# Two transformer layers on one core: heads paired in the score units, attention normalized by VectorE transposes, the bias b2 added on GpSimd, and planner latencies taken from a trace

## The chip, the cores and the metric

The kernel runs on one core of one Trainium2 chip. The metric is the device time of one execution in microseconds (us); lower is better. Each kernel was timed several times in rounds shared with the kernel before; quoted times are medians.

TensorE is the matmul engine, VectorE, ScalarE and GpSimd the others. In profile lines they are PE (PEld its weight loads), DVE, ACT and POOL; SP or SPq is the queue that issues DMAs. PSUM (ps in profile lines) is the memory, in banks, that holds what matmuls write. The granted clock is the share of TensorE's full clock that the profile shows as granted.

## The reference, cut to what matters

```python
def _A_ref(x, wqkv, wo):                 # x: 1 x 2048 x 512, 32 heads of 16, window 256
    q, k, v = split(x @ wqkv)
    scores = einsum("bhqd,bhkd->bhqk", q, k) * 16 ** -0.5
    scores = where(0 <= q_index - k_index < 256, scores, -1e9)
    return (softmax(scores) @ v) @ wo
def _B_ref(x, w1, b1, w2, b2):           # 512 -> 1792 -> 512
    return gelu(x @ w1 + b1) @ w2 + b2
x = x + _A_ref(layernorm(x), ...)        # both layers twice, the same weights
x = x + _B_ref(layernorm(x), ...)
```

## The kernel before

The Python program first records some thousand operations with their data dependencies, then a planner (`_Plan.run`) simulates the five engines with assumed durations and latencies. Its greedy list schedule gives the order in which every engine gets its instructions. On the chip the order is fixed; only semaphores decide when the next instruction starts. So a number in the planner changes no operation, but may change the order of all of them.

```python
class _Plan:
    LAT = {"pe": 230.0, "act": 110.0, "dve": 110.0, "pool": 150.0, "sp": 100.0}   # ns to a dependent
    # in run():  pick the ready operation of best priority whose PSUM banks are free
    #            dur += 98.0 at a mode switch of TensorE, += 1283.0 at a table load of ScalarE
    # ... (cut)
```

Scores are computed in units of 320 queries by 128 keys of one head; the two PSUM halves hold two halves of 64 keys. Probabilities times V (PV) then leaves two partial sums, one for each half, in two PSUM banks. Each V carries a 17th column of ones, so its row 16 is the softmax denominator. The normalization follows:

```python
# reduce: adds the two banks, PSUM -> SBUF
add("dve", e.tensor_reduce(out=OD[:, s], in_=ps[:, two banks].rearrange("p b n -> p n b"), op=ALU.add), ...)
dma(Dc[:, rs] <- OD[Dh : P : 32, s])                 # gather the denominators
add("dve", e.reciprocal(Rc[:, rs], Dc[:, rs]), ...)
dma(scr_r[rs] <- Rc[:, rs])                          # to DRAM
dma(Rn[:, rs] <- scr_r[rs] broadcast to 16 rows)     # and back, one row for each of 16
for r in range(4):
    dma(OD[32*r+16 : 32*r+32, s, 0] <- OD[32*r : 32*r+16, s, 1])   # move the odd heads
add("pool" or "dve", e.tensor_tensor(out=OT[:, bs, c], in0=OD[:, s, 0], in1=Rn[:, rs], op=ALU.mult), ...)
# ... OT feeds the out-projection, then residual, layernorm, MLP
```

The bias b2 is one more matmul (a row of ones times b2) in each of the 32 groups of the second MLP product; then VectorE adds X and PSUM. The mask multiply runs on VectorE or GpSimd, as the planner chooses.

The softmax here doesn't subtract the row's maximum and nothing guards it: scores larger than these inputs give would overflow.

## Time and profile before

557.39 us median (557.38 with the execution that was added when the change was timed). Of the profiled execution:

| what | before |
|---|---|
| span of the profiled run | 551.9 us |
| TensorE busy; span less busy | 484.1; 67.8 us |
| ScalarE, VectorE, GpSimd busy | 423.6, 385.9, 271.1 us |
| granted TensorE clock, mean | 0.969 |

The page of the kernel before, from its first part and from the chain of work that ended last (shares of the span):

```profile
span 551.9 us, 20560 instructions
## 1 busy us (share of the span) xinstructions
PE 484.1 (88%) x9040; PEld 247.1 (45%) x9040; DVE 385.9 (70%) x669; ACT 423.6 (77%) x507; POOL 271.1 (49%) x359
...
PE 39%; DMA 18%; DVE 18%; SPq 12%; ACT 9%; issue 3%; POOL 1%; DVEq 0%; POOLq 0%
```

TensorE is the fullest engine, and yet 30% of the chain is DMA and DMA issue. The middle of the kernel before, 60 to 500 us, by windows (busy us of each engine, instruction counts, granted clock, DMA share):

```profile
core 0: us, PE busy (x) PEld busy (x) DVE busy (x) ACT busy (x) POOL busy (x), PEclk, DMA share, GB/s
60.00:500.00 440.00, 394.41 (x7772) 195.90 (x7773) 320.54 (x557) 356.86 (x416) 229.16 (x272) 0.97 0.12 33
```

The groups of instructions of the kernel before that the change touches (busy us, mean ns of one, idle time before them and what ended it):

```profile
L692 POOL TENSOR_TENSOR E<-E,mask 128x512 bf16<-128x512 bf16 x163 | 192.1, 1187 | 147.1 <-ACT E L678 147.1
L737 DVE TENSOR_REDUCE OD<-ps 128x512 f32<-128x1024 f32 x64 | 77.9, 1217 | 14.9 <-PE ps L726 14.4
...
L754 POOL TENSOR_TENSOR OT<-OD,Rn 128x256 bf16<-128x256 f32 x34 | 25.2, 741 | 61.9 <-DMA Rn<-scr_r 56.8 <-DMA OD<-OD 5.1
L744 DVE RECIPROCAL Rc<-Dc 64x32 f32<-64x32 f32 x64 | 21.6, 338 | 28.6 <-DMA Dc<-OD 28.5
...
L757 DVE TENSOR_TENSOR OT<-OD,Rn 128x256 bf16<-128x256 f32 x30 | 16.0, 534 | 26.8 <-DMA Rn<-scr_r 21.3 <-DMA scr_r<-Rc 3.7 <-DMA OD<-OD 1.8
```

The normalization costs VectorE 77.9 + 21.6 + 16.0 = 115.5 us. The waits of the kernel before that end at the normalized tile OT (us in total, times, longest):

```profile
PEld ps L564 <- POOL OT L754: 8.2, 5, 3.3
...
PE ps L564 <- POOL OT L754: 6.9, 5, 3.2
```

The chain of the last attention group of the kernel before, in order of time (start us, us, what), shows the latency itself:

```profile
516.24 1.80 DMA Dc<-OD
...
518.13 1.43 SPq L751
...
522.14 2.71 DMA Rn<-scr_r
...
524.97 0.43 DVE OT L757
```

The reduce of that group starts at 514.8 us, and the out-projection at 525.46. Only part of this is transfer: from 518.13 to 522.1 us the chain consists of five DMA issues that stand one behind the other in SP's queue, about 4 of the 11 us. The Trainium skill, "DMA: Bandwidth & Descriptors" (Anatomy of one DMA), gives a DMA issued by GpSimd a fixed cost of about 2.0 us, most of it waiting for the write to be confirmed; the DMAs here are issued by SP, and the two pieces, 1.80 and 2.71 us, are of that size.

### The profile page before, as it was taken

How to read it: one execution, taken by the hardware profiler on the slowest of the kernel's cores; microseconds unless marked ns; L12 is line 12 of the kernel's file. 1: busy time of each engine (PE TensorE's matmuls, PEld its weight loads, DVE VectorE, ACT ScalarE, POOL GpSimd, SP SyncE). 2: the span in 40 equal slices, each digit the busy share in tenths (PEclk: the TensorE clock that was granted, in tenths of full speed). 3: DMA queues.
4: the chain of work that ended last, by engine and by line, in shares of the span. 5: the costliest groups of instructions: out<-in, count | busy, mean ns of one | idle time of the engine just before them, and what ended most of it. 6: DMA issues, size and time to landing. Idle time of an engine off the chain costs nothing.

```text
span 551.9 us, 20560 instructions
## 1 busy us (share of the span) xinstructions
PE 484.1 (88%) x9040; PEld 247.1 (45%) x9040; DVE 385.9 (70%) x669; ACT 423.6 (77%) x507; POOL 271.1 (49%) x359
## 2 busy tenths in 40 slices
PE   3895788989878997998998999998999998969997
PEld 2553454545433542545444453445434443434653
DVE  5997986868687666856788686786766675863331
ACT  2788798889877894798869987589757996788542
POOL 6575664646584335643566457562553344532010
PEclk9998799999979997998999999999999999979999
DMA  8901111010111011100111101110111102110100
GB/s 275 297 17 41 43 27 40 23 34 20 36 45 33 14 25 38 37 24 11 37 35 33 30 14 42 34 29 15 45 53 43 32 9 61 45 45 25 51 20 30
DMA packets 37131, 24.93 MB, mean 45 GB/s; under 512 B 16305, under 2 KB 36530, under 8 KB 37042
## 3 DMA queue, kind: packets, MB, share of 16 engines
q1 hardware_dynamic: 37042, 23.62, 14.6%
q8 instruction: 71, 1.16, 0.9%
q14 instruction: 18, 0.15, 0.1%
HBM read 16.26 MB, written 2.62 MB: 34 GB/s over the span
## 4 chain that ended last, share of the span: by engine, by line
PE 39%; DMA 18%; DVE 18%; SPq 12%; ACT 9%; issue 3%; POOL 1%; DVEq 0%; POOLq 0%
PE ps L564 30%; SPq L751 9%; DMA Dc<-OD 7%; DMA Rn<-scr_r 6%; ACT E L678 5%; DMA scr_r<-Rc 5%; DVE OD L737 4%; PE ps L665 4%; PE ps L726 3%; DVE KT L608 2%; DVE E L689 2%; DVE X L573 2%; ACT gT L826 1%; SPq L748 1%; PE ps L548 1%
## 5 line engine op out<-in xcount | busy, mean ns | idle before, releaser
L678 ACT ACTIVATE E<-ps 128x1024 bf16<-128x1024 f32 x320 | 303.6, 1039 | 65.4 <-PE ps L665 65.0
L692 POOL TENSOR_TENSOR E<-E,mask 128x512 bf16<-128x512 bf16 x163 | 192.1, 1187 | 147.1 <-ACT E L678 147.1
L564 PE MATMUL ps<-xnTB,W_sb 128*128 128x512 bf16 (+1 forms) x560 | 114.5, 339 | 7.9 <-DVE gT L814 3.9
L564 PE MATMUL ps<-W_sb,gT 128*128 128x512 bf16 x448 | 120.2, 383 | 0.0
L737 DVE TENSOR_REDUCE OD<-ps 128x512 f32<-128x1024 f32 x64 | 77.9, 1217 | 14.9 <-PE ps L726 14.4
L665 PE MATMUL ps<-QT,KT 32*64 32x320 bf16 (+4 forms) x3072 | 69.8, 265 | 15.5 <-ACT E L678 9.4
L564 PE MATMUL ps<-xnTA,Wqkv_sb 128*128 128x256 bf16 x512 | 70.5, 281 | 6.3 <-DVE xnTA L517 1.7
L564 PEld LDWEIGHTS ps<-xnTB,W_sb 128*128 128x128 bf16 x560 | 50.2, 98 | 51.1 <-DVE gT L814 6.8
L573 DVE TENSOR_TENSOR X<-X,ps 128x512 bf16<-128x512 bf16 x64 | 43.2, 676 | 38.7 <-PE ps L564 38.6
L826 ACT ACTIVATE gT<-ps,b1T 128x512 bf16<-128x512 f32 (+1 forms) x92 | 50.4, 584 | 18.6 <-PE ps L564 18.4
L689 DVE TENSOR_TENSOR E<-E,mask 128x512 bf16<-128x512 bf16 x93 | 53.0, 572 | 14.4 <-ACT E L678 13.7
L665 PEld LDWEIGHTS ps<-QT,KT 32*64 32x64 bf16 x3072 | 29.0, 104 | 69.7 <-ACT E L678 36.0
L564 PEld LDWEIGHTS ps<-W_sb,gT 128*128 128x128 bf16 x448 | 37.7, 98 | 45.2 <-issue 14.7
L726 PE MATMUL ps<-E,Va 64*17 64x192 bf16 (+3 forms) x3840 | 52.2, 238 | 6.5 <-DVE E L689 2.7
L564 PEld LDWEIGHTS ps<-xnTA,Wqkv_sb 128*128 128x128 bf16 x512 | 46.3, 100 | 24.0 <-issue 3.3
L726 PEld LDWEIGHTS ps<-E,Va 64*17 64x17 bf16 x3840 | 42.5, 87 | 29.6 <-issue 13.0
L754 POOL TENSOR_TENSOR OT<-OD,Rn 128x256 bf16<-128x256 f32 x34 | 25.2, 741 | 61.9 <-DMA Rn<-scr_r 56.8
L564 PE MATMUL ps<-Wo_sb,OT 128*128 128x512 bf16 x128 | 36.2, 419 | 9.3 <-POOL OT L754 6.9
L608 DVE TENSOR_TENSOR KT<-ps,parmask 128x1024 bf16<-128x1024 f32 x32 | 38.6, 1213 | 6.8 <-PE ps L564 6.6
L530 DVE BATCH_NORM_STATS2 stat<-X 128x6 f32<-128x512 bf16 x64 | 42.8, 679 | 0.5
L744 DVE RECIPROCAL Rc<-Dc 64x32 f32<-64x32 f32 x64 | 21.6, 338 | 28.6 <-DMA Dc<-OD 28.5
L564 PE MATMUL ps<-Wqkv_sb,xnTA 128*128 128x512 bf16 x128 | 35.4, 393 | 5.1 <-DVE KT L608 3.3
(46 smaller groups left out, 360.8 us busy)
## 6 DMA issues: line engine op xcount, KB each, us to landing
Rn<-scr_r SPq DMA_DIRECT2D x64, 128.0 KB
OD<-OD SPq DMA_DIRECT2D x256, 16.0 KB
W_sb<-in_B_w_dram SPq DMA_DIRECT2D x2, 1792.0 KB
out_dram<-X SPq DMA_DIRECT2D x16, 128.0 KB
Wqkv_sb<-in_A_wqkv_dram SPq DMA_DIRECT2D x3, 512.0 KB
X<-in_A_x_dram SPq DMA_DIRECT2D x1, 1024.0 KB
Dc<-OD SPq DMA_DIRECT2D x64, 8.0 KB
scr_r<-Rc SPq DMA_DIRECT2D x64, 8.0 KB
```

Of the source, the lines that this page charges most:

```text
L530: add("dve", lambda e, B: e.bn_stats(stat6[:, k6, :], X[:, t, :]), 680, reads=["X%d" % t], writes=["st%d" % k6], prio=prio)
L564: r = e.matmul(ps[:, B[g][0], cols], lhsT, rhs, start=st, stop=sp)
L573: add("dve", lambda e, B: e.tensor_tensor(out=X[:, t, :], in0=X[:, t, :], in1=ps[:, B[g][0], :], op=ALU.add), d_psum(512), reads=["X%d" % ...
L608: add("dve", lambda e, B, g=g, i=i: e.tensor_tensor(out=KT[:, kb, :, 2 * i : 2 * i + 2, :].rearrange("p a c q -> p a (c q)"), in0=ps[:, B[ ...
L665: x = e.matmul(ps[HK * h : HK * h + HK, bk[r], o : o + n], KT[rows, kb, par, c, j * P + HK * h : j * P + HK * h + HK], QT[rows, c, q + HK ...
L678: a = (add("act", lambda e, B, g_=g_, gi=gi: e.activation(E[:, 2 * gi : 2 * gi + 2, e0 : e0 + 512], ps[:, B[g_][0] : B[g_][0] + 2, :], AF. ...
L689: add("dve", lambda e, B: e.tensor_tensor(out=Ew, in0=Ew, in1=Mw, op=ALU.mult), d_bf2(8 * HK * n), reads=["E%d%s" % (es, x) for es in ess ...
L692: alt=(("pool", lambda e, B: e.tensor_tensor(out=Ew, in0=Ew, in1=Mw, op=ALU.mult), POOL_M * n, POOL_H),))
L726: x = e.matmul(ps[32 * r : 32 * r + VW, B[g][half], par * 256 + q_lo * HK : par * 256 + q_hi * HK], lhsT, rhs, start=(pi == 0), stop=(pi = ...
L737: add("dve", lambda e, B: e.tensor_reduce(out=OD[:, s, :, :].rearrange("p a q -> p (a q)"), in_=ps[:, B[g][0] : B[g][0] + 2, :].rearrange( ...
L751: dma(lambda e, B, r=r: e.dma_start(OD[32 * r + Dh : 32 * r + 2 * Dh, s, 0, :], OD[32 * r : 32 * r + Dh, s, 1, :]), [ods[r]], reads=["Dc%d ...
L826: gelu_last[0] = add("act", lambda e, B, g=g, fc=fc: e.activation(gT[:, fc, 0:M], ps[:, B[g][0], 0:M], AF.Gelu_apprx_tanh, bias=b1T[:, fc ...
```

## The change

The intent is (N) a normalization without DMA, (B) no b2 matmuls on TensorE, and (P) a planner whose latencies come from a trace.

N: a score unit now holds 64 keys of an even head in one PSUM half and of the odd head in the other, so a head's sum over keys stays in one bank and nothing has to be added. V is also stored with its halves swapped (`Vs`, 64 DMA copies), because the odd head's 64 keys may lie in the other 64 rows. The 64 matmuls by zeros with which the old PV opened some of its sums are gone too. PV's output is transposed in 32x32 blocks by VectorE; then a denominator lies beside its 16 values in one partition, is inverted and multiplied there, and the result is transposed back.

```diff
-  e.tensor_reduce(OD, two banks); dma Dc<-OD; e.reciprocal(Rc, Dc); dma scr_r<-Rc; dma Rn<-scr_r; 4 x dma OD<-OD
-  add("pool", OT = OD * Rn, alt "dve")
+  add("dve", e.transpose(OD[:, s, :], ps[:, two banks, 0:256]), 715, ...)
+  sums = OD[:, s, :].rearrange("p (a k n) -> p a k n", a=2, n=32)
+  add("dve", e.reciprocal(Rc[:, s, :], sums[:, :, :, Dh]), 205, ...)
+  add("dve", Nb = sums[:, :, :, 0:Dh] * Rc broadcast, 360, lock=True, alt=(("pool", norm, 741, 0.0, True),))
+  add("dve", e.transpose(OT[:, bs, c, :], Nb[:, s, :]), 420, ...)
... (score and PV loops by head parity, Vs copies: cut)
```

B:

```diff
-  pe_group(g, [(onesb, b2row, ...)] + [(gT, W2_sb, ...) for fc in range(FC)], ...); residual: X = X + ps
+  add("pool", Xb = X + b2all, 1180, ..., lock=True)
+  pe_group(g, [(gT, W2_sb, ...) for fc in range(FC)], ...);  add("dve", X = Xb + ps, 690, ...)
```

P:

```diff
-    LAT = {"pe": 230.0, "act": 110.0, "dve": 110.0, "pool": 150.0, "sp": 100.0}
+    OVER = {"pe": 0.0, "act": 105.0, "dve": 82.0, "pool": 42.0, "sp": 0.0}      # overlap with the next
+    LAT = {"pe": {"pe": 0.0, "act": 204.0, "dve": 204.0, "pool": 230.0, "sp": 230.0},
+           "act": {"pe": 57.0, ...}, "dve": {"pe": 57.0, ...}, "pool": {...}, "sp": {...}}
+    SWITCH = 96.0;  TABLE = 1400.0
+    # lock=True: such operations of VectorE and GpSimd are kept apart in the plan
... (durations of a dozen operations adjusted by up to 110 ns: cut)
```

## The prediction

> **What bounds the kernel now.** TensorE and ScalarE hold each other. The page gives TensorE 484 of 551.9 us busy (88%), ScalarE 424, VectorE 386, GpSimd 271. Cut into windows: from 60 to 500 us TensorE is busy 394 of 440 us and ScalarE 397, both near 90%; from 0 to 60 TensorE only 41.5 (in 30 to 60 VectorE is the full one, 26.8 of 30); from 500 to 552 TensorE works almost alone (48 of 52). So 45 us of TensorE idle in the middle, 18 at the start and 4 at the end can be attacked. The waits view names them: weight loads of the scores waiting for exp 36 us, ScalarE waiting for scores 65 us, TensorE (weight loads and matmuls) waiting for the normalized tile 15 us. The chain of waits puts 18% on DMA and 12% on DMA issue: sums -> reciprocal -> DRAM -> broadcast -> multiply. At 206.6 us the timeline shows TensorE standing 3.2 us for that.
>
> **What changes, costed from the trace.**
> - Normalization: VectorE now spends 64 x 1217 ns (reduce) + 64 x 338 (reciprocal) + 30 x 534 (multiply) = 115 us; GpSimd 25. After: a transpose out of PSUM, estimated at the 677 ns of the 512-column cast, a reciprocal about 0.2, a bf16 transpose about 0.42, a multiply of 0.4 to 0.53, half of them on GpSimd at 741: about 97 us. The Trainium skill, "VectorE: DVE Perf Modes" (Rules for kernel authors), calls tensor_reduce the slowest VectorE op and the 32x32 transpose the fastest within a bank; the trace agrees on the reduce. VectorE gains 15 to 20 us.
> - Latency from PV to out-projection: about 11 us (last block: reduce starts 514.8, out-projection 525.5) becomes 2 to 3. Its 448 DMAs vanish; 64 V-swap copies come, mostly hidden.
> - TensorE: 32 b2 matmuls at about 0.21 us (estimate: spacing of 512-column matmuls in the timeline) and 64 zero matmuls: minus 8 us. Scores and PV keep counts and columns; pairing heads instead of key halves should not change their speed.
> - GpSimd: plus 32 x about 1.18 us (like its 512-element mask multiply, 1187 ns), so about 305 us busy; some masks go to VectorE. A busier GpSimd also delays VectorE's SBUF operations (mask multiply there averages 572 ns).
> - Planner: order from traced latencies, costed only as a share of the 45 us.
>
> **On the critical path.** DMA latency mostly hides behind other blocks' work; only the stalls count: about 10 us in the middle, 2 to 3 at the start, 3 at the end. TensorE work: 7 of 8 counts. Better order: 8 to 10. ScalarE's 424 us stays, so the middle can't fall far below 410. Sum about 31 us: 526.
>
> **Predicted:** 526 us, range 508 to 545. Chances: faster 0.87, same 0.11, slower 0.02.
>
> **What would show it right.** TensorE busy falls to about 474 and its share rises to 90% or more; DMA leaves the chain; VectorE busy 365 to 375, GpSimd about 305; ScalarE within 10 us of 424; middle ScalarE idle below 8%; out-projection waits near zero; transpose near 0.7 us.
>
> **What would make it wrong.** GpSimd's b2 adds and normalizations delay the tiny layernorm operations on it or slow VectorE, so masks and PV slip; V-swap copies arrive late at the first blocks; the new order has more TensorE mode switches or starves ScalarE; the clock (0.969 now) falls as TensorE gets denser. In the other direction: if the old order was the true cause of the gaps, under 510.

## More of the kernel before

One early execution of the kernel before took 1516.97 us; it is in no ratio, and without it the median of the kernel before would be 557.36 instead of 557.38.

The experiments ran in three rounds on different chips, in which the kernel before took 558.05, 555.28 and 555.44 us, so kernels of different rounds are better compared by their ratios than by their medians.

Pairing in the trace the end of each of the 64 reduces with the end of the matching write of OT gives a median of 11.0 us from PSUM eviction to normalized tile.

## The result, and the profile after

The kernel after takes 538.08 us median (533.73 to 539.45) against 557.38: ratio 0.9655, interval [0.9597, 0.9714]. A ratio here is the mean time of one kernel's fast runs over that of the kernel before in the same rounds, so it is not quite the ratio of the medians quoted. The predicted time was 526, so the range holds the result; of the predicted gain of 31 us, 19 came.

The page of the kernel after, the same parts:

```profile
span 535.7 us, 19845 instructions
## 1 busy us (share of the span) xinstructions
PE 472.1 (88%) x8944; PEld 254.8 (48%) x8944; DVE 387.3 (72%) x739; ACT 427.4 (80%) x514; POOL 292.4 (55%) x376
...
PE 60%; DVE 18%; ACT 18%; issue 2%; POOL 2%; POOLq 0%; DVEq 0%
```

DMA has left the chain, and TensorE's busy time fell by 12.0 us. But the span less TensorE's busy time only went from 67.8 to 63.6 us, and VectorE is as busy as before. The groups of the kernel after that answer to those above:

```profile
L747 DVE STREAM_TRANSPOSE OD<-ps 128x512 f32<-128x512 f32 x64 | 45.4, 710 | 17.2 <-PE ps L737 15.7
...
L837 POOL TENSOR_TENSOR Xb<-X,b2all 128x512 f32<-128x512 bf16 x32 | 37.7, 1179 | 44.3 <-DVE X L841 29.8 <-DVE X L594 14.6
...
L760 DVE STREAM_TRANSPOSE OT<-Nb 128x256 bf16<-128x256 bf16 x64 | 27.8, 434 | 2.4 <-POOL Nb L754 2.0
...
L754 POOL TENSOR_TENSOR Nb<-OD,Rc 128x256 bf16<-128x256 f32 x33 | 22.7, 687 | 9.3 <-DVE Rc L750 8.4 <-DVE statmv L553 0.8
...
L754 DVE TENSOR_TENSOR Nb<-OD,Rc 128x256 bf16<-128x256 f32 x31 | 19.5, 628 | 0.5
...
L750 DVE RECIPROCAL Rc<-OD 128x16 f32<-128x16 f32 x64 | 15.4, 240 | 0.2
```

The normalization now costs VectorE 45.4 + 27.8 + 19.5 + 15.4 = 108.1 us, only 7 less than before. The waits of the kernel after that end at OT:

```profile
PEld ps L585 <- DVE OT L760: 0.9, 4, 0.2
PEld ps L691 <- DVE OT L760: 0.4, 1, 0.4
```

No stall at the out-projection is longer than 0.2 us, where it was 3.3. The same pairing in the trace gives a median of 2.9 us from eviction to normalized tile, where it was 11.0. The middle by windows:

```profile
core 0: us, PE busy (x) PEld busy (x) DVE busy (x) ACT busy (x) POOL busy (x), PEclk, DMA share, GB/s
60.00:500.00 440.00, 399.46 (x7972) 210.88 (x7949) 328.41 (x623) 374.11 (x437) 246.03 (x283) 0.96 0.05 13
```

The mean granted clock was 0.958 (0.969 before), and in the timed runs 0.955 to 0.965.

### The profile page after: what moved, and what is told of

It reads as the page before. It is cut to its first block, busy times and chain, and to the rows that moved or that the text cites. A ratio compares the mean times of both kernels' runs of the same rounds, so it can differ in the third digit from the quotient of the medians.

```text
span 535.7 us, 19845 instructions
## 1 busy us (share of the span) xinstructions
PE 472.1 (88%) x8944; PEld 254.8 (48%) x8944; DVE 387.3 (72%) x739; ACT 427.4 (80%) x514; POOL 292.4 (55%) x376
## 4 chain that ended last, share of the span: by engine, by line
PE 60%; DVE 18%; ACT 18%; issue 2%; POOL 2%; POOLq 0%; DVEq 0%
PE ps L585 46%; ACT E L704 12%; PE ps L737 6%; PE ps L691 6%; DVE KT L629 3%; DVE xn L561 2%; DVE stat L551 2%; ACT gT L820 2%; DVE E L715 2%; PE ps L569 2%; DVE OD L747 2%; DVE gT L817 1%; ACT L820 1%; DVE X L841 1%; DVE X L594 1%
## 5 line engine op out<-in xcount | busy, mean ns | idle before, releaser
L718 POOL TENSOR_TENSOR E<-E,mask 128x512 bf16<-128x512 bf16 x151 | 177.3, 1182 | 143.4 <-ACT E L704 143.1
L585 PE MATMUL ps<-W_sb,gT 128*128 128x512 bf16 x448 | 114.9, 380 | 0.3 <-DVE X L841 0.3
L715 DVE TENSOR_TENSOR E<-E,mask 128x512 bf16<-128x512 bf16 x105 | 66.0, 632 | 27.0 <-ACT E L704 26.8
L691 PE MATMUL ps<-QT,KT 32*64 32x320 bf16 (+4 forms) x3072 | 70.2, 267 | 14.8 <-ACT E L704 8.5
L837 POOL TENSOR_TENSOR Xb<-X,b2all 128x512 f32<-128x512 bf16 x32 | 37.7, 1179 | 44.3 <-DVE X L841 29.8
L747 DVE STREAM_TRANSPOSE OD<-ps 128x512 f32<-128x512 f32 x64 | 45.4, 710 | 17.2 <-PE ps L737 15.7
L737 PE MATMUL ps<-E,Va 64*17 64x64 bf16 (+3 forms) x1920 | 51.0, 240 | 5.8 <-ACT E L704 3.0
L737 PE MATMUL ps<-E,Vs 64*17 64x64 bf16 (+3 forms) x1920 | 51.7, 240 | 0.0
L841 DVE TENSOR_TENSOR X<-Xb,ps 128x512 bf16<-128x512 f32 x32 | 21.8, 681 | 34.1 <-PE ps L585 33.9
L569 PE MATMUL ps<-ident,xn 128*128 128x128 bf16 x256 | 25.9, 230 | 20.3 <-DVE xn L561 9.8
L561 DVE TENSOR_SCALAR xn<-X,statmv,rstd 128x512 bf16<-128x512 bf16 x64 | 41.5, 653 | 2.7 <-POOL rstd L558 2.5
## 6 DMA issues: line engine op xcount, KB each, us to landing
W_sb<-in_B_w_dram SPq DMA_DIRECT2D x2, 1792.0 KB, 14.8
```

The source lines that it names most:

```text
L561: add("dve", lambda e, B: e.tensor_scalar(out=xn[:, s, :], in0=X[:, t, :], scalar1=statmv[:, k, 0:1], scalar2=rstd[:, k : k + 1], op0=ALU. ...
L585: r = e.matmul(ps[:, B[g][0], cols], lhsT, rhs, start=st, stop=sp)
L691: x = e.matmul(ps[HK * par : HK * par + HK, bk[r], o : o + n], KT[rows, kb, par, c, m * HK : m * HK + HK], QT[rows, c, q : q + n], start=T ...
L715: add("dve", lambda e, B: e.tensor_tensor(out=Ew, in0=Ew, in1=Mw, op=ALU.mult), 355 * n, reads=["E%d%s" % (es, x) for es in ess for x in " ...
L718: alt=(("pool", lambda e, B: e.tensor_tensor(out=Ew, in0=Ew, in1=Mw, op=ALU.mult), POOL_M * n, POOL_H, True),))
L737: x = e.matmul(ps[32 * r : 32 * r + VW, B[g][par], q_lo * HK : q_hi * HK], V[rows, (2 * b + m // 2) % VR, c * HC + 2 * r + par, :], E[rows ...
```

## The experiments

The three parts can be separated: N, B and P each on or off makes eight kernels, two of which are before and after. Five of the other six were run. Because the order of all instructions follows from the planner's numbers, controls nudge one number, the planner's cost of a TensorE mode switch, by 4 ns. No operation changes, but every engine gets another order (over a thousand lines of difference in VectorE's and TensorE's lists for the kernel after). Idle is the profiled span less TensorE's busy time; a dash stands where the trace lacks about 100 of TensorE's records, so that its busy time is too small to use. One profiled execution stands for each kernel: that of the kernel before (span 551.9 us) was among its fastest, that of norm_only (device time 536.22 us) its slowest, so differences of idle carry an error of some 3 us.

| kernel | N | B | P | median us | ratio to before | TensorE busy | idle | clock |
|---|---|---|---|---|---|---|---|---|
| before | – | – | – | 557.38 | 1 | 484.1 | 67.8 | 0.969 |
| before_jitter | – | – | – | 552.82 | 0.9931 | 483.4 | 70.6 | 0.975 |
| b2_only | – | yes | – | 552.55 | 0.9924 | 474.4 | 77.0 | 0.966 |
| norm_only | yes | – | – | 533.95 | 0.9594 | 481.3 | 53.0 | 0.981 |
| no_planner | yes | yes | – | 528.82 | 0.9496 | 471.7 | 55.4 | 0.971 |
| no_planner_jitter | yes | yes | – | 528.34 | 0.9506 | 470.2 | 56.7 | 0.977 |
| planner_only | – | – | yes | 567.07 | 1.0169 | 490.9 | 75.1 | 0.948 |
| planner_only_jitter | – | – | yes | 564.87 | 1.0167 | – | – | 0.964 |
| b2_back_on_pe | yes | – | yes | 550.15 | 0.9865 | 484.3 | 64.6 | 0.969 |
| after | yes | yes | yes | 538.08 | 0.9655 | 472.1 | 63.6 | 0.958 |
| after_jitter | yes | yes | yes | 526.99 | 0.9471 | 468.3 | 56.3 | 0.971 |
| after_jitter2 | yes | yes | yes | 525.69 | 0.9458 | – | – | 0.964 |
| before_no_dma | wrong result | – | – | 532.44 | 0.9571 | – | – | 0.981 |
| norm_with_hops | yes, slowed | – | – | 545.78 | 0.9813 | – | – | 0.974 |

Half-widths of the 95% intervals are 0.003 to 0.008.

### planner_only: P alone

```diff
  (kernel before)
- old planner class and durations
+ new planner class, its durations, overlaps and locks
```

> The kernel before with the new planner (traced latencies, overlaps, port locks, durations) alone; normalization by DMA and b2 on TensorE stay. Theory of the prediction (three parts that add): 8 to 10 us faster than before, 547 to 550. Rival 1 (the gain is the removed TensorE work, the order is only noise): within 4 us of before, 553 to 561. Rival 2 (the order is the whole gain): 535 to 542.

Measured: 567.07 us, ratio 1.0169 [1.0116, 1.0221]. None of the three theories expected a loss. On the operations of the kernel before, the new planner costs 9 us instead of gaining 8 to 10.

### no_planner: N and B without P

```diff
  (kernel after)
- new planner class and durations
+ old planner class and durations
```

> The kernel after with the old planner and its old durations; paired heads, transposes and b2 on GpSimd stay. Theory of the prediction: gives back 8 to 10 us, 546 to 549. Rival 1 (removed TensorE work is the gain, order is noise): 536 to 542, TensorE busy about 472. Rival 2 (the order is the whole gain): 553 to 560.

Measured: 528.82 us, 0.9496 [0.9444, 0.9549]. All three theories were wrong in time: without the new planner the changed kernel is faster, by about 1.6% in the ratios. N and B together gain 5.0%, some 28 us, nearly the 31 that were predicted for all three.

### b2_back_on_pe: N and P without B

```diff
  (kernel after)
- add("pool", Xb = X + b2all); X = Xb + ps
+ one b2 matmul in each of the 32 groups; X = X + ps
```

> The kernel after with b2 as 32 matmuls again, no GpSimd add. Theory of the prediction: 7 us slower than after, 545, TensorE busy up by 7 to 12 us, GpSimd busy down by 38. Rival 1 (removed TensorE work is the gain): 8 to 12 us slower, 546 to 550. Rival 3 (the GpSimd adds cost about what the matmuls did, by delaying VectorE and the layernorm): within 3 us of after, 535 to 541, VectorE's mean mask multiply back below 600 ns.

Measured: 550.15 us, 0.9865, TensorE busy 484.3: 12.2 more than after, GpSimd's 258.6 us are 33.8 less. B's gain in this pair, 12 us or 2.1%, equals the busy time removed; rival 1 (546 to 550) comes nearest. Rival 3 predicted under 541 and has no support here: the GpSimd adds did not cost what the matmuls did. But these are two single orders, and orders differ by as much (see the controls), so the pair alone decides little. VectorE's mean mask multiply did not return below 600 ns (637). The adds are not what lengthens it: with them alone (b2_only) it is 574 ns, as before (572); with the new normalization alone (norm_only) it is 662.

### b2_only: B alone

```diff
  (kernel before)
- one b2 matmul in each of the 32 groups; X = X + ps
+ add("pool", Xb = X + b2all); X = Xb + ps
```

> The kernel before with b2 on GpSimd alone. Theory of the prediction: 7 us faster, 550. Rival 1: 8 to 12 us faster, 545 to 549. Rival 3 (GpSimd contention eats it): within 3 us of before, 554 to 560.

Measured: 552.55 us, 0.9924 [0.9873, 0.9975]: 0.8%, 4 us, between the bands of the theory and of rival 3, though TensorE's busy time fell by 9.7 us. Idle rose from 67.8 to 77.0: in this pair half of the removed work (by the medians) or nearly all of it (by the profiles) came back as waiting. Between norm_only and no_planner the same part is worth 0.9594 against 0.9496, 1.0% or some 5.5 us; there busy fell by 9.6 and idle rose by only 2.4. Between b2_back_on_pe and after it is worth 2.1%, and idle did not rise at all (64.6 to 63.6). All three pairs have the same sign, but none is clearly larger than what a change of order alone does (before_jitter 0.7%, the orders of the kernel after 2%). So B is worth 4 to 12 us, and these runs don't tell it closer.

### norm_only: N alone

```diff
  (kernel after)
- new planner, b2 on GpSimd
+ old planner, b2 on TensorE
```

> The kernel before with paired heads and DMA-free normalization alone (old planner, b2 on TensorE). The four runs so far read: b2 on GpSimd gains 5.5 to 12, the new planner costs 9, the normalization gains 17 or more. If the parts add: 528.8 + 5.5 to 12 = 534 to 541. Rival (the normalization's gain is an accident of one order): over 547. TensorE busy about 481 to 484; VectorE busy no lower than 380.

Measured: 533.95 us, 0.9594 [0.9526, 0.9662], inside the additive band. Alone it gains 4.1%, 21 to 23 us, at least as much as the whole change (the intervals of the two ratios overlap). With B already there it gains 4.3% (b2_only to no_planner), under the new planner 3.0% (planner_only to b2_back_on_pe). TensorE's busy time fell by only 2.8 us; its idle time fell by 14.8 (67.8 to 53.0). VectorE's busy time is 387.7 us, 1.8 more than before.

### before_jitter, after_jitter, no_planner_jitter, planner_only_jitter, after_jitter2: the controls

```diff
- mode switch 98 (old planner) or 96 (new planner) ns
+ 94 (before_jitter), 102 (no_planner_jitter), 92 (after_jitter, planner_only_jitter), 100 (after_jitter2)
```

> Control: the kernel before with its mode switch 94 instead of 98 ns. If the constants of the kernel before were tuned to one order, every other order is slower: 560 to 570, and then the 9 us of the new planner alone are the loss of that tuning. If the order is not special: 554 to 560.

> Control: the kernel after with one planner constant nudged, TensorE's mode switch 92 instead of 96 ns; same operations and same costs on the chip, but another order on every engine. If the planner's model is what costs 9 us, this stays at 535 to 541. If the spread of orders is as large as the effect, it lands anywhere in 528 to 548, and the 9 us are not the model's.

> Control: the fast run with the old planner, its mode switch 102 instead of 98 ns. If the old model is really better on the changed kernel: 525 to 533. If 528.8 was a lucky order: 534 or more, as the kernel after.

> Control: the kernel before with the new planner, its mode switch 92 instead of 96 ns. If the new model really fits the old operations worse: 562 to 570. If 567 was an unlucky order, as 538 was for the changed kernel: 548 to 560.

> Control: the kernel after with the mode switch at 100 instead of 96 ns. If 538 was an unlucky order and 527 the usual one: 524 to 532. If orders spread evenly: anywhere in 526 to 542.

Measured: 552.82 (0.9931 [0.985, 1.0012]), 526.99 (0.9471), 528.34 (0.9506), 564.87 (1.0167) and 525.69 us (0.9458). (A first try of no_planner_jitter at 94 ns could not be built: the planner ran into a state where no PSUM bank came free.) Three readings follow.

First, 538.08 us is an unlucky order: two other orders of the same operations under the same model take 526 to 527 us, 11 to 12 less (10 to 11 by the ratios), far outside the spread of the executions of either. The kernel before, nudged, is not slower (below both its bands), so it was not tuned to one best order.

Second, on the changed kernel the two models do not differ in what these orders can tell: 528.8 and 528.3 with the old one; 538.1, 527.0 and 525.7 with the new one. The conclusion drawn from no_planner alone, that the new model costs 9 us there, falls.

Third, on the old operations both orders of the new model are 1.7% slower, so there the loss is probably more than luck, though two orders against two do not prove it. With N and b2 on TensorE the new model is slower too (norm_only 0.9594, b2_back_on_pe 0.9865), one order each. Why it is so was not found.

What an unlucky order looks like: the kernel after by windows around a starved stretch.

```profile
core 0: us, PE busy (x) PEld busy (x) DVE busy (x) ACT busy (x) POOL busy (x), PEclk, DMA share, GB/s
180.00:217.60 37.60, 35.44 (x652) 18.18 (x650) 26.11 (x54) 33.06 (x41) 20.01 (x27) 1.00 0.04 10
217.60:231.30 13.70, 9.21 (x302) 5.46 (x295) 8.48 (x16) 12.52 (x14) 6.70 (x8) 0.51 0.01 2
231.30:252.00 20.70, 20.13 (x245) 10.07 (x243) 14.07 (x29) 17.45 (x21) 6.57 (x10) 0.99 0.04 8
```

From 217.6 to 229 us the order gives TensorE nothing but scores and PV: no matmul of a projection or of the MLP runs in that time. ScalarE's exp is then the limit (busy for 11.15 of these 11.4 us), TensorE is busy for only 6.91 and waits for exp or for what follows it, and the mean granted clock is 0.51. The waits of TensorE there, from 217.6 to 229 us of the kernel after:

```profile
PE ps L691 <- ACT E L704: 1.1, 1, 1.1
PE ps L737 <- DVE E L715: 1.1, 1, 1.1
PE ps L691 <- DVE OD L747: 0.9, 1, 0.9
...
```

The nearest full windows of the two orders, 180 to 240 us, differ in the same way, first the kernel after, then after_jitter:

```profile
core 0: us, PE busy (x) PEld busy (x) DVE busy (x) ACT busy (x) POOL busy (x), PEclk, DMA share, GB/s
180.00:240.00 60.00, 53.35 (x1095) 27.48 (x1094) 42.58 (x85) 52.70 (x61) 32.28 (x40) 0.89 0.03 7
180.00:240.00 60.00, 56.52 (x1145) 28.83 (x1144) 45.57 (x87) 53.34 (x64) 40.03 (x47) 1.00 0.05 12
```

Over the whole kernel after_jitter's span is 11.1 us shorter: 7.3 us less idle and 3.8 us less busy, with the clock at 0.971 for 0.958. The stretch at 217.6 us is not the whole of it: these 60 us differ by 3.2 us of TensorE's busy time, and other windows differ as much, without a halved clock too (300 to 320 us: busy 15.69 us after, 18.47 after_jitter; 420 to 440: 15.83 and 19.54). How the 11 us divide among the stretches was not measured.

### before_no_dma: the old normalization without its DMAs (wrong result)

```diff
  (kernel before)
- dma Dc<-OD; dma scr_r<-Rc; dma Rn<-scr_r; 4 x dma OD<-OD
+ Dc and Rn are filled once with constants; reduce, reciprocal and multiply stay and wait for each other
```

> Wrong result on purpose: the kernel before with the normalization's seven DMAs per group taken out (reciprocal and multiply read constants, the odd heads are not moved), while the reduce, the reciprocal and the multiply stay on their engines. Theory A (what the new normalization gains is the DMA latency between PV and out-projection): 533 to 542, TensorE idle (span less busy) down from 68 to 52 to 58 us. Rival B (it gains by shorter VectorE work: transpose for reduce): 552 to 558.

Measured: 532.44 us, 0.9571 [0.9533, 0.961]; the relative error of 21.6 is intended. Theory A holds in time (0.6 us under its band); its number for idle can't be read, because the trace lacks records. From the groups of before_no_dma:

```profile
L738 DVE TENSOR_REDUCE OD<-ps 128x512 f32<-128x1024 f32 x64 | 78.0, 1218 | 13.1 <-PE ps L727 12.0
```

VectorE still does the full reduces (78.0 us), and is busy 389.6 us in all, and yet the whole gain of norm_only (0.9594) is there. So the shorter VectorE operations are not needed to explain it. Rival B falls. (The planner knew of the missing DMAs, so the order is another one too; the gain, 4.3%, is larger than any difference between two orders here, 2%.) From eviction to normalized tile the trace has a median of 1.95 us.

### norm_with_hops: the new normalization with latency put back

```diff
  (norm_only)
- e.transpose(OT, Nb)
+ dma N2<-Nb; dma scr_n<-N2; dma N3<-scr_n; e.transpose(OT, N3)
```

> Correct result: the normalization-only kernel (533.95 us) with three DMA hops in a row put back between the multiply and the last transpose, by way of DRAM, some 7 us per group; VectorE's new operations stay. Theory A: most of the 21 us come back, 546 to 556. Rival B: stays at 531 to 538.

Measured: 545.78 us, 0.9813 [0.9768, 0.9857], 0.2 us under theory A's band and far from B's. From the DMA issues of norm_with_hops (KB each, median us from issue to landing):

```profile
N<-Nb SPq DMA_DIRECT2D x64, 64.0 KB, 1.8
scr_n<-N SPq DMA_DIRECT2D x64, 64.0 KB, 1.5
N<-scr_n SPq DMA_DIRECT2D x64, 64.0 KB, 1.8
```

Eviction to normalized tile has a median of 9.5 us again (2.6 in norm_only), and about 12 of the 21 us come back. Here TensorE stands at OT for only 1.1 us of weight-load waits, so the latency mostly works at a distance: a late out-projection makes residual, layernorm and the MLP late, whose matmuls TensorE lacks elsewhere. That path was argued, not isolated. Why 9.5 us cost 12 and the old kernel's 11.0 some 21 is open; one order each, and orders differ by up to 12. One candidate stands in the waits: in the kernel before, VectorE stood 55.4 us (28.6 + 26.8 in the groups above) and GpSimd 61.9 us before operations that waited for these DMAs, and whatever came next in their fixed order stood behind them; in norm_with_hops VectorE stood 14.9 us and GpSimd not at all. No run tests it.

## Why the prediction was right or wrong

The forecast of "faster" and the range were right; the gain was 19 us instead of 31. Term by term:

1. **"TensorE work: 7 of 8 counts" — not contradicted, not resolved.** TensorE's busy time fell by 12.0 us, to 472.1 (predicted 474). B is worth 4 to 6 us under the old planner (ratio 0.9924; 0.9594 to 0.9496) and 12 under the new one (0.9865 to 0.9655). How much of the removed work came back as idle time differs as widely between the three pairs, from nearly all to none, and differences of order are as large.

2. **"About 10 us in the middle, 2 to 3 at the start, 3 at the end" for the stalls — the right cause, counted too small.** Removing the latency is worth 21 to 23 us (norm_only), and before_no_dma shows that it is the latency. "Only the stalls count" was wrong. The 15 us of waits in the prediction counted the same stalls twice, at the weight load and at the matmul; the direct stalls were about 10 us (8.2 us at GpSimd's tiles, 1.7 at VectorE's). Most of the gain is therefore not in stalls that the waits view puts down to the tile. The latency itself was predicted well: 11 to 2 to 3; measured 11.0 to 2.9.

3. **"Better order: 8 to 10" — this step failed.** I credited the new planner with a gain in advance because its numbers are closer to a trace. On the old operations it loses 9 us in two orders of two, where 8 to 10 of gain were forecast. On the changed ones the order that was shipped is about 9 us slower than the old planner's, and 11 to 12 slower than two other orders from the same model. With about 22.5 for N and 5.5 for B (4.1% and 1.0% of 555), 28 us are there without the planner (528.82, measured directly); the shipped order gives back 9, and 19 remain.

4. **"VectorE gains 15 to 20 us", busy 365 to 375 — wrong, and it did not matter.** VectorE is busy 387.3 us. The transpose was sized well (710 ns for an estimate of 677), but the reciprocal took 240 ns for 200 and the multiply 628 ns for 400 to 530: 108 us instead of 97. (The 0.2 and 0.42 us of the prediction are the planner's durations in the diff above, 205 and 420 ns; the second held, at 434.) Twelve more masks went to VectorE (105 for 93), and layernorm's scaling rose from 531 to 653 ns. The Trainium skill, "SBUF — State Buffer" (SBUF: two separate sides), says that VectorE and GpSimd share a port pair that one instruction holds alone while the other fully blocks; a VectorE instruction with two inputs in SBUF, as the mask multiply is, meets it against a GpSimd one that reads SBUF. The trace of the kernel after fits: the mask multiply on VectorE takes 354 ns at the least, 426 in the median and 1393 at the most, while one GpSimd multiply takes 1182. No run isolates it. "VectorE: DVE Perf Modes" (Rules for kernel authors) calls the reduce the slowest VectorE operation and VectorE the fastest way to transpose 32x32 within a bank. No run here compares ways to transpose, and this trace does not set the reduce apart: the old reduce took 1217 ns for 1024 columns, the mask multiply of K out of PSUM 1213 for as many. The transpose saves because it reads 512 columns instead of 1024; its 710 ns lie above the 677 of a plain cast of as many. None of this is where the gain came from (before_no_dma keeps the reduce).

5. **"ScalarE 397 of 440, both near 90%" — a misreading.** The windows say 356.86 of 440, 81%. ScalarE stayed within 10 us in all (427.4), as predicted, but its middle idle share is 15%, not below 8%, and no floor of 410 us for the middle follows from it. GpSimd was predicted at 305 and is at 292.4. TensorE's share stayed at 88%, not 90.

6. **"The clock falls as TensorE gets denser" — it fell, but not for density.** The densest kernel without lost records, norm_only at 90%, had the highest clock of its runs, 0.981 to 0.987, and planner_only, at 87%, the lowest, 0.948 to 0.955.

A version that beats both kernels is therefore N and B in any of the four other orders that were run: for instance, after_jitter2 at 525.69 us and no_planner at 528.82 give the right result and are 2.0% and 1.6% faster than the kernel after, by their ratios.

## What to carry to other kernels

Where a program computes its order from a cost model, one measured time is one draw: nudge a constant that changes no operation, two or three times, before you credit or blame the model. Price a latency by running the kernel without it, on constants if need be, rather than by adding up the waits that name it; here the direct stalls came to about 10 us and the removal gave 22. And read TensorE as busy plus idle: work taken from an engine that waits for others can come back as idle time, here between all and none of it.

## What the Trainium skill lacked or had wrong

- "TensorE: Matmul & The Clock Gate" (What's actually happening; HAM oscillation): it ties the half clock to an idle window of about 3.4 us and advises against idle gaps longer than that. A later passage (A second HAM failure mode) lets frequent micro-idles between groups of matmuls do it too, but gives no size. In the kernel after the mean granted clock was 0.51 from 217.6 to 231.3 us, about four such windows, though the longest wait of TensorE from 217.6 to 229 us was 1.1 us; only small-tile scores and PV ran in that time, TensorE busy 6.91 of 11.4 us. So a long idle gap was not needed here, which fits the later passage; which mix of short waits and small matmuls brings the half clock on, no run here tells.
- "VectorE: DVE Perf Modes" (The three transpose paths) gives a time for a block transpose of bf16 only. Here a 128x512 f32 transpose out of PSUM takes 710 ns and a 128x256 bf16 one in SBUF 434 ns.
- "SBUF — State Buffer" (SBUF: two separate sides) gives factors from separate probes, but no spread of durations inside a mixed kernel. Here, where the lock is the suspected and untested cause, the VectorE mask multiply spreads from 354 to 1393 ns, and the layernorm scaling from 325 to 1345 ns.
- No page says how much a fixed order varies: 4 ns in one planner constant moved the time by 11 us of 538.
